# Attention and mixture of experts on one Trainium2 core: how often a place of TensorE's order issues a gather of rows

## The chip, the cores and the metric

One core of a Trainium2 chip runs the whole kernel. The metric is the time of one execution on the device in microseconds. The engines have an instruction stream each and meet through semaphores: TensorE (PE, with its weight loads as PEld), VectorE (DVE), ScalarE (ACT), GpSimd (POOL) and SyncE (SP). GpSimd and SyncE issue the transfers here.

## The reference

Attention over 8 batches of 8 heads of 576 tokens, each with a causal window of 32 (or every fourth of 128), then a mixture of 8 experts in which a token either takes its own best expert or that of the token before it:

```python
attn = softmax(mask(q @ k.T / 8)) @ v                     # B, H, S, D = 8, 8, 576, 64
x = attn.transpose(0, 2, 1, 3).reshape(B, S, 512)
logits = x @ w_gate                                       # 8 experts
local_gate = sigmoid(x @ w_local)
for b in range(B):
    prev_e = -1
    for s in range(S):
        fresh_e = argmax(logits[b, s])
        e = fresh_e if s == 0 or local_gate[b, s] < 0.5 else (prev_e if prev_e >= 0 else fresh_e)
        prev_e = e
        p = softmax(logits[b, s])
        out[b, s] = p[e] * (relu(x[b, s] @ w1[e]) @ w2[e])    # 512 -> 1024 -> 512
```

## The kernel before

Attention comes first and writes the tokens' rows x to device memory, in the tensor xd. The routing then sorts the tokens by expert into tables. The rest of the kernel works through a fixed list of 19 **units**, each a group of tokens of one expert, whose size is the unit's kind: pair (2 x 128 tokens), quad (4 x 128 = 512), full (128), half (64) and quart (32). Units 0 to 3 are pairs; from unit 4 on the list is full, half, **quad (6)**, quart (7), **quad (8)**, full (9), **quad (10)**, half, quart, **quad (13)**, full, **quad (15)**, quart, **quad (17)**, quart.

A unit passes through these steps:

- `weights(u, second)`: SyncE loads the expert's w1 or w2 (2 MB, tile raw, L916) into the slot u % 2, once the unit that held the slot has been through that product. If the expert is the one already held there, the load is skipped.
- `gather(u)` puts the unit's gathers in the list `fetches`; a quad has 16 of them, 4 for each of its 4 tiles xg of 128 tokens. `fetch` issues one: a memset of a single element on VectorE, which claims the tile (L999), then an indirect transfer of 128 rows of 128 values, issued by GpSimd (L1000). There are 9 tiles xg, and `gather_more` puts a unit in the list only when its tiles are free.
- `features(u)`: all gathers of the unit that are still in the list are issued (`fetch_all`); then VectorE transposes each xg into a tile xe (L1037) and forms four sums of those for a quad (tile xcq, L964 to L967).
- `hidden(u)`: the first product. A pair and a quad do it in seven half-size products rather than eight (Strassen's scheme in Winograd's form), for which VectorE forms sums of the weights (tile sum) and afterwards adds parts of the results (L1195 for a quad).
- `output(u)`: the second product (L1293), in the same seven products, once for each half of a quad, with sums of h in the tile hc (L958 to L961). VectorE and ScalarE scale the results by the gate into the tiles y (L1309, L1302, L1306), and GpSimd scatters them to the output (`send`, L1222; L1243 for a half, L1261 for a quart).

The order on TensorE and VectorE is the program's own; no scheduler moves anything there. The main loop runs, for u from 2 on, `hidden(u)`, then `features(u + 1)`, then `output(u - 1)`. `hidden` and `output` are generators that yield at **places** between TensorE's products; a quad's hidden part has 14 places and its output 14. At each place `work_gap` issues up to two pending VectorE operations from the list `soon`, and then `gap(time)` calls `fetch_some(time)`, the credit that sets how often a gather is issued:

```python
def fetch_some(time):
    since[0] = min(since[0] + time, 5)
    cost = 2 if fetches and FIRST <= fetches[0][0] <= TURNED else 3
    if fetches and since[0] >= cost:
        since[0] -= cost
        fetches.pop(0)[1]()
```

For units behind unit 4 a gather costs 3. A place of a pair or a quad gives 2, a place of a smaller unit 1.

Of the kernel before, what the change touches and what calls it, by code (L numbers as in the profile page):

```python
# [218 lines left out]
def whole(ctx, tc, exact, bad, qk, v, wgl, w1, w2, con, msk, qmk, out, cst, wg, ones):  # L219
# [664 lines left out]
    units = [dict(kind="pair", col=2 * i, late=False) for i in range(FIRST)]  # L884
# [15 lines left out]
    def weights(u, second):  # L900

        i = units[u]["slot"]
        loads.add((u, second))
        if not second:
            units[u]["held"] = holds.get(i)
            holds[i] = nc.values_load(of_unit(u, "experts", rows=1), engines=[ET.SP], min_val=0, max_val=E - 1,
                                      skip_runtime_bounds_check_because="clamped to the experts")
            units[u]["expert"] = holds[i]
        e, held = units[u]["expert"], units[u]["held"]
        w, s, pattern = (w2, raw2, "p m f -> p (m f)") if second else (w1[u >= TURNED], raw1, "p m k f -> p (m k f)")  # L910
        if not second and u >= TURNED and units[u]["before"] < TURNED:
            held = None
        if second and not units[u]["late"] and isinstance(held, int):
            held = None
        more = {} if held is None else dict(cond=e != held, cond_hint=False)
        nc.sync.dma_start(out=s[i].rearrange(pattern), in_=w[bass.ds(e, 1)].rearrange("o p x -> (o p) x"), **more)  # L916
# [6 lines left out]
    def next_weights(*did):  # L923

        ready.update(did)
        if "late" in ready:
            for w in [w for w in follow if w in ready]:
                follow.remove(w)
                weights(after[w[0]], w[1])

    def gap(time=3):
        fetch_some(time)
        for steps in waiting, behind:
            if steps:
                f = steps.pop(0)
                if f:
                    f()

    def work_gap(sums=True, time=2):
        for _ in range(len(soon) > 4 and 2 or len(soon) > 0 if sums else 0):  # L940
            soon.pop(0)()
        gap(time)
# [5 lines left out]
    def flush():  # L948
        while soon:
            soon.pop(0)()  # L950
# [18 lines left out]
    def sums_of_weights(u, second):  # L969

        i = units[u]["slot"]
        assert (u, second) in loads
        if second:
            return sums_right(sums[1], *(quarter(raw2[i], k, j, True) for k in range(2) for j in range(2)))
        return sums_left(sums[0], *(quarter(raw1[i], f, k, False) for f in range(2) for k in range(2)))
# [50 lines left out]
    def turn_rows(u):  # L1026
        kind = units[u]["kind"]
        rows = {"half": ROW, "quart": SQ}.get(kind, P)
        assert u >= TURNED or kind == "pair"
        fetch_all(u)  # L1030
        xe[u] = [mw.tile([P, DK, 2 * P], F32, name="xe") for _ in range(2 if kind == "quad" else 1)]
        for j in range({"quad": 4, "pair": 2}.get(kind, 1)):
            x = xg.pop((u, j))
            to = xe[u][j // 2][:, :, j % 2 * P:j % 2 * P + rows]
            if u >= TURNED:
                x = x.rearrange("p g (q f) -> p (g q) f", f=P)
                nc.vector.transpose(to.rearrange("p k (q t) -> p k q t", t=SQ),  # L1037
                                    x[:, :rows // SQ].rearrange("p q (k d) -> p k q d", k=DK))
                continue
            x = x.rearrange("p g f -> p (g f)")  # L1040
            tp = bank([P, DK, P], "tp")
            for kk in range(DK):
                nc.tensor.transpose(tp[:, kk], x[:, kk * P:(kk + 1) * P], ident)
            nc.scalar.copy(to, tp)
# [159 lines left out]
    def turned(u):  # L1204

        h = ht[u]
        n = 2 if units[u]["kind"] == "half" else 1
        ts = h[:, 0:n].rearrange("p m t -> p (m t)")
        tp = bank([P, 2 * n, P], "ht")
        for c in range(2 * n):  # L1210
            nc.tensor.transpose(tp[:, c], ts[:, c * P:(c + 1) * P], ident)
        nc.scalar.copy(h[:, 2:2 + n].rearrange("p m (c t) -> p (m c) t", t=P), tp)
# [244 lines left out]
    def run_hidden(u, push):  # L1457
        soon.extend(push)
        for k, fits in enumerate(hidden(u)):
            work_gap(fits, 2 if is_large(u) else 1)  # L1460
            if u == FIRST and k == 1:
                early_sums[u] = sums_of_weights(u, True)
                soon.extend(early_sums[u][:2])
            if u == FIRST and k == 4:
                turn_rows(u + 1)
        flush()
        if u < FIRST:
            next_weights((u, False))
        elif after[u] is not None:
            weights(after[u], False)  # L1470

    def run_output(u, push):
        soon.extend(push)
        for k, fits in enumerate(output(u)):
            work_gap(fits, 2 if is_large(u) else 1)
            if u == NU - 2 and k == 4:
                turned(u + 1)
        if u == NU - 2 and k < 4:
            turned(u + 1)
        flush()  # L1480
        if u < FIRST:
            next_weights((u, True))
        elif after[u] is not None:
            weights(after[u], True)

    def is_large(u):
        return FIRST <= u < NU and units[u]["kind"] in ("pair", "quad") or 0 <= u < FIRST
# [20 lines left out]

    early_sums[0] = sums_of_weights(0, True)
    run_hidden(0, early_sums[0][:2])  # L1510
    features(1)
    now(both(0))
    run_output(0, [])
    run_hidden(1, sums_of_weights(1, True))
    now(units[1]["sums"])
    fed = False
# [19 lines left out]
    for u in range(FIRST, NU):  # L1536
        own = is_large(u) and u >= TURNED and before_it(u) < u - 1
        run_hidden(u, (both(u - 1) if u > FIRST else []) + (wait(5) + sums_of_weights(u, True) if own else []))
        if u > FIRST and u + 1 < NU:
            features(u + 1)  # L1540
        gather_more(min(u + 1, NU - 1) if u > FIRST else FIRST)
        push = [f for t in when.get(u, []) for f in
                wait((7 if units[u - 1]["kind"] == "quad" else 5) if is_large(u - 1) else 0) + sums_of_weights(t, False)]
        if u > FIRST:
            run_output(u - 1, push)
        else:
            now([f for two_ in zip(sums_of_rows(u + 1), sums_of_weights(u + 1, False)) for f in two_])
        if units[u]["kind"] in ("half", "quart") and u < NU - 1:
            turned(u)
        if u in (FIRST + 3, FIRST + 4) and not exact:  # L1550
            next(checks)
        if u == FIRST + 6 and not exact:
            again = register(bad[0:1, 0:1], 1, "a comparison's result")
    now(both(NU - 1))
    run_output(NU - 1, [])
    return again

# [58 lines left out]
```

## Time and profile before

| | |
|---|---|
| median of 3 runs | 641.37 us (640.75 to 643.07) |
| profiled execution, its own time | 645.84 us |
| span of the profiled execution | 643.9 us |
| PE busy | 604.5 us, 94% of the span |
| PEld busy | 511.2 us, 79% |
| DVE busy | 360.5 us, 56% |
| POOL busy | 226.0 us, 35% |
| ACT busy | 176.2 us, 27% |
| mean granted clock of TensorE | 0.983 of full |
| moved by DMA | 121.18 MB, mean 188 GB/s |

Busy shares are means over stages that are limited by different things. In a row of a timeline stand the start, the duration, the engine, the line and operation, what is written and read, the count of instructions merged in the row, and in square brackets the engine's idle time ahead of it with what ended it. In a row of a stretch of time (A:B) stand its length, then busy time with the count for PE, PEld, DVE, ACT and POOL, then the granted clock, the mean share of the 16 DMA engines, and GB/s; a row for one tile alone leaves out an engine that has nothing to do with it.

### The profile page before, as it was taken

The page shows a single profiled execution, that of the slowest core. Times are in us where ns is not written, and L with a number is a line of the kernel's source. Part 1 is how long each engine was busy: PE and PEld are TensorE (multiplying, and loading weights), DVE is VectorE, ACT ScalarE, POOL GpSimd, SP SyncE. Part 2 cuts the span into 40 slices and gives each one's busy share as a digit, 9 for nine tenths or more (in the row PEclk, how much of TensorE's full clock was granted, in tenths as well). Part 3 has the DMA queues.
Part 4 walks back from the last instruction along what each step waited for, and adds up shares of the span by engine and source line. Part 5 has one row for each costly group of instructions (what it writes and reads, how often), then busy time and mean ns, then how long its engine had stood idle before and what let it go on. Part 6 is the DMA issues. An engine that isn't in the chain of part 4 may idle for free.

```text
span 643.9 us, 13952 instructions
## 1 busy us (share of the span) xinstructions
PE 604.5 (94%) x5678; PEld 511.2 (79%) x5678; DVE 360.5 (56%) x902; ACT 176.2 (27%) x320; POOL 226.0 (35%) x219
## 2 busy tenths in 40 slices
PE   6879988879999998999979999999999999999995
PEld 6767777668888998868768898868789888688884
DVE  3757889989697384374344464434445535443521
ACT  2555544342211331113112311221132113112310
POOL 3232142223014644463256335444543451011011
PEclk8989989999999999999979999999999999999998
DMA  9989988398001247251835192454554650734131
GB/s 348 406 319 294 346 278 299 122 344 342 15 34 35 82 161 262 84 202 26 351 122 188 49 387 76 174 175 164 167 206 160 285 188 31 274 159 163 43 127 42
DMA packets 28442, 121.18 MB, mean 188 GB/s; under 512 B 4748, under 2 KB 15116, under 8 KB 22992
## 3 DMA queue, kind: packets, MB, share of 16 engines
q1 hardware_dynamic: 20800, 101.04, 42.9%
q0 software_dynamic: 7568, 19.15, 8.8%
q8 instruction: 47, 0.77, 0.5%
q14 instruction: 27, 0.22, 0.1%
HBM read 120.17 MB, written 19.14 MB: 216 GB/s over the span
## 4 chain that ended last, share of the span: by engine, by line
PE 79%; DVE 10%; issue 4%; DMA 3%; ACT 1%; POOL 1%; SPq 1%; another core or an unknown queue 0%; DVEq 0%; POOLq 0%
PE yp L1293 29%; PE hp L1179 23%; PE hp L1121 3%; PE pv L410 3%; PE yp L1269 3%; PE hp L1147 3%; PE sc L348 3%; PE hp L1136 2%; PE tp L429 2%; DVE pr L354 2%; DVE x L415 1%; PE yp L1253 1%; PE yp L1234 1%; PE hp L1098 1%; DMA vt<-in_v_dram 1%
## 5 line engine op out<-in xcount | busy, mean ns | idle before, releaser
L1000 POOL DMA_INDIRECT xg<-xd,at x116 | 117.8, 1015 | 144.4 <-DVE xg L999 115.8
L1293 PE MATMUL yp<-sum,hc 128*128 128x256 f32 x384 | 88.7, 380 | 1.6 <-ACT y L1302 1.6
L1293 PEld LDWEIGHTS yp<-sum,hc 128*128 128x128 f32 x384 | 72.7, 190 | 11.8 <-ACT y L1302 2.0
L1222 POOL DMA_INDIRECT out_dram<-y,tok x35 | 43.5, 1242 | 97.3 <-DVE y L1309 43.3
L1309 DVE SCALAR_TENSOR_TENSOR y<-yp,gate,y 128x256 f32<-128x256 f32 x48 | 23.1, 484 | 89.9 <-PE yp L1293 62.1
L1179 PE MATMUL hp<-xcq,sum 128*128 128x256 f32 x288 | 64.1, 379 | 0.0
L1293 PE MATMUL yp<-raw,h 128*128 128x256 f32 x256 | 62.0, 386 | 0.0
L1179 PEld LDWEIGHTS hp<-xcq,sum 128*128 128x128 f32 x288 | 54.7, 190 | 7.4
L357 ACT ACTIVATE pr<-pr 128x512 f32<-128x512 f32 x64 | 43.8, 684 | 60.0 <-DVE pr L354 56.9
L1293 PEld LDWEIGHTS yp<-raw,h 128*128 128x128 f32 x256 | 48.7, 193 | 8.6 <-issue 2.0
L354 DVE SCALAR_TENSOR_TENSOR pr<-sc,mk 128x512 f32<-128x512 f32 x64 | 45.4, 748 | 16.9 <-PE sc L348 15.4
L410 PE MATMUL pv<-vt,pr 128*64 128x65 f32 x1152 | 44.9, 231 | 9.8 <-issue 5.8
L410 PEld LDWEIGHTS pv<-vt,pr 128*64 128x64 f32 x1152 | 39.3, 143 | 13.2 <-issue 7.7
L1195 DVE TENSOR_TENSOR h<-hp,h 128x512 f32<-128x512 f32 x36 | 24.3, 689 | 41.8 <-PE hp L1179 41.8
L1179 PE MATMUL hp<-xe,raw 128*128 128x256 f32 x192 | 43.4, 379 | 0.0
L1179 PEld LDWEIGHTS hp<-xe,raw 128*128 128x128 f32 x192 | 36.2, 190 | 4.8
L1302 ACT ACTIVATE y<-yp,gate 128x256 f32<-128x256 f32 x48 | 22.7, 474 | 61.7 <-PE yp L1293 54.4
L348 PE MATMUL sc<-kq 64*64 64x96 f32 (+3 forms) x1280 | 34.3, 246 | 5.2 <-DVE pr L354 2.8
L289 POOL COPY vt<-vt 64x1040 f32<-64x1040 f32 x16 | 17.3, 1080 | 57.6 <-DMA vt<-in_v_dram 38.8
L348 PEld LDWEIGHTS sc<-kq 64*64 64x64 f32 x1280 | 28.8, 136 | 10.7 <-DVE pr L354 4.0
L1000 POOL DMA_INDIRECT xg<-xd,row x16 | 18.2, 1140 | 52.9 <-DVE xg L999 20.6
L1306 ACT ACTIVATE y<-yp,gate 128x256 f32<-128x256 f32 x16 | 7.6, 475 | 105.7 <-PE yp L1293 105.7
(261 smaller groups left out, 976.6 us busy)
## 6 DMA issues: line engine op xcount, KB each, us to landing
raw<-in_w_dram SPq DMA_DIRECT2D x38, 2048.0 KB
kq<-in_qk_dram SPq DMA_DIRECT2D x13, 1184.0 KB
vt<-in_v_dram SPq DMA_DIRECT2D x15, 650.0 KB
xd<-x SPq DMA_DIRECT2D x16, 512.0 KB
kq<-in_qk_dram SPq DMA_DIRECT2D x6, 592.0 KB
xg<-xd,at POOLq DMA_INDIRECT x116
xd<-x SPq DMA_DIRECT2D x32, 32.0 KB
vt<-in_v_dram SPq DMA_DIRECT2D x2, 325.0 KB
```

The costliest lines, as they stand in the source:

```text
L348: nc.tensor.matmul(sc[c:c + QB, u, lo - a * QB:hi - a * QB], lhsT=kt[h, WIN + j * QB:WIN + (j + 1) * QB], rhs=qt[h, lo:hi], start=True, st ...
L354: nc.vector.scalar_tensor_tensor(to, sc[:, :, :w], -CEIL, mk[:, at:at + w].unsqueeze(1).to_broadcast([P, 2, w]), Alu.max, Alu.min)
L357: nc.scalar.activation(to, to, Act.Exp, scale=SCALE)
L410: nc.tensor.matmul(pv[half * QB:(half + 1) * QB, k - a], lhsT=pr[:, u, (i - a) * QB:(i - a + 1) * QB], rhs=vt[:, slot(i), u], start=True, ...
L1000: nc.gpsimd.indirect_dma_start(out=to, out_offset=None, in_=of, in_offset=bass.IndirectOffsetOnAxis(ap=place, axis=0))
L1121: nc.tensor.matmul(to, lhsT=w[:, m, kk], rhs=x[:, kk, :P], start=(kk == 0), stop=(kk == DK - 1))
L1179: nc.tensor.matmul(to[v][:, m], lhsT=a[:, 2 * v + m, kk], rhs=b[:, kk], start=first and m == 0 and kk == 0, stop=(kk == DK // 2 - 1), skip ...
L1195: nc.vector.tensor_tensor(to, of[v], to, op=Alu.add)
L1222: nc.gpsimd.indirect_dma_start(out=rows_of_out(), out_offset=bass.IndirectOffsetOnAxis(ap=of_unit(u, "tok", j), axis=0), in_=y, in_offset= ...
L1293: nc.tensor.matmul(to, lhsT=a[:, m], rhs=b[:, m], start=first and m == 0, stop=(m == FK // 2 - 1), skip_group_check=True)
L1302: nc.scalar.activation(at(k), of, Act.Copy, scale=of_unit(u, "gate", 2 * s + k // 2))
L1309: nc.vector.scalar_tensor_tensor(at(k), of, of_unit(u, "gate", 2 * s + k // 2), at(k), Alu.mult, Alu.add)
```

## The change

A place of a quad now gives a credit of 3 instead of 2, so that at each of a quad's places one gather is issued while there are any in the list. Places of other kinds are as before.

```diff
     def run_hidden(u, push):
         soon.extend(push)
         for k, fits in enumerate(hidden(u)):
-            work_gap(fits, 2 if is_large(u) else 1)
+            work_gap(fits, 3 if units[u]["kind"] == "quad" else 2 if is_large(u) else 1)
...
     def run_output(u, push):
         soon.extend(push)
         for k, fits in enumerate(output(u)):
-            work_gap(fits, 2 if is_large(u) else 1)
+            work_gap(fits, 3 if units[u]["kind"] == "quad" else 2 if is_large(u) else 1)
```

The order of TensorE, ScalarE and SyncE is the same in both kernels. On VectorE the memsets of L999 move, on GpSimd the gathers of L1000 among the sends. In the rows below a number behind a tile's name tells its buffers apart; they count differently in the two kernels.

VectorE in the second half of unit 6's hidden part (the first quad), before. The tiles xg_3516, xg_3557 and xg_3604 are unit 8's second, third and fourth; xe_3619 is unit 7's.

```order
L999 MEMSET xg_3557 1x1
L967 TENSOR_TENSOR sum_1_2490<-raw2_0_78,sum_1_2490 128x1024
L1195 TENSOR_TENSOR h_3505<-hp_3506,h_3505 128x2x256
L1195 TENSOR_TENSOR h_3505<-hp_3507,h_3505 128x2x256
L999 MEMSET xg_3557 1x1 x2
L1195 TENSOR_TENSOR h_3505<-hp_3508,h_3505 128x2x256
L1195 TENSOR_TENSOR h_3505<-hp_3509,h_3505 128x2x256
L999 MEMSET xg_3604 1x1 x2
L1037 STREAM_TRANSPOSE xe_3619<-xg_3428 128x4x32
L999 MEMSET xg_3604 1x1
```

The same place now; here xg_3545 and xg_3580 are unit 8's third and fourth tiles, and xg_3613 is unit 9's.

```order
L999 MEMSET xg_3545 1x1
L967 TENSOR_TENSOR sum_1_2490<-raw2_0_78,sum_1_2490 128x1024
L999 MEMSET xg_3580 1x1
L1195 TENSOR_TENSOR h_3505<-hp_3506,h_3505 128x2x256
L1195 TENSOR_TENSOR h_3505<-hp_3507,h_3505 128x2x256
L999 MEMSET xg_3580 1x1 x2
L1195 TENSOR_TENSOR h_3505<-hp_3508,h_3505 128x2x256
L1195 TENSOR_TENSOR h_3505<-hp_3509,h_3505 128x2x256
L999 MEMSET xg_3580 1x1
L999 MEMSET xg_3613 1x1 x2
L1037 STREAM_TRANSPOSE xe_3628<-xg_3428 128x4x32
L999 MEMSET xg_3613 1x1 x2
```

Unit 8's last memset now stands right behind unit 6's last L1195, and four of unit 9's follow it. Before, unit 8's fourth tile had three of its four here.

VectorE a little later, at unit 8's `features`, before (xe_3682 and xe_3683 are unit 8's):

```order
L958 TENSOR_TENSOR hc_2492<-h_3505 128x512
L959 TENSOR_TENSOR hc_2492<-hc_2492,h_3505 128x512
L999 MEMSET xg_3604 1x1
L960 TENSOR_TENSOR hc_2492<-h_3505 128x512
L961 TENSOR_TENSOR hc_2492<-h_3505,hc_2492 128x512
L1037 STREAM_TRANSPOSE xe_3682<-xg_3448 128x4x128
L1037 STREAM_TRANSPOSE xe_3682<-xg_3516 128x4x128
L1037 STREAM_TRANSPOSE xe_3683<-xg_3557 128x4x128
L1037 STREAM_TRANSPOSE xe_3683<-xg_3604 128x4x128
```

The same place now:

```order
L958 TENSOR_TENSOR hc_2492<-h_3505 128x512
L959 TENSOR_TENSOR hc_2492<-hc_2492,h_3505 128x512
L960 TENSOR_TENSOR hc_2492<-h_3505 128x512
L961 TENSOR_TENSOR hc_2492<-h_3505,hc_2492 128x512
L1037 STREAM_TRANSPOSE xe_3691<-xg_3448 128x4x128
L1037 STREAM_TRANSPOSE xe_3691<-xg_3516 128x4x128
L1037 STREAM_TRANSPOSE xe_3692<-xg_3545 128x4x128
L1037 STREAM_TRANSPOSE xe_3692<-xg_3580 128x4x128
```

No memset stands between hc's sums any more.

GpSimd over the same stretch, from the end of unit 4's output to unit 6's output, before:

```order
L1000 DMA xg<-xd,at 128x128 x4
L1222 DMA out_dram<-y,tok_2889 4608x512
L1000 DMA xg<-xd,at 128x128 x11
L1243 DMA out_dram<-y,side 9216x256
L1000 DMA xg<-xd,at 128x128 x4
L1222 DMA out_dram<-y,tok_2889 4608x512
```

And now:

```order
L1000 DMA xg<-xd,at 128x128 x4
L1222 DMA out_dram<-y,tok_2889 4608x512
L1000 DMA xg<-xd,at 128x128 x16
L1243 DMA out_dram<-y,side 9216x256
L1000 DMA xg<-xd,at 128x128 x5
L1222 DMA out_dram<-y,tok_2889 4608x512
```

Sixteen gathers are issued ahead of the half unit's scatter (L1243, unit 5) where eleven were; unit 8's last was the first behind that scatter, and is now the twelfth of the sixteen.

VectorE from the weights' sums in unit 6's output to those at the start of unit 8's hidden part, before (the end of that stretch):

```order
L959 TENSOR_TENSOR sum_0_79<-sum_0_79,raw1_0_77 128x1024
L999 MEMSET xg_3762 1x1
L1309 SCALAR_TENSOR_TENSOR y_3756<-yp_3752,gate1_2899,y_3756 128x256
L999 MEMSET xg_3762 1x1
L1309 SCALAR_TENSOR_TENSOR y_3755<-yp_3753,gate1_2899,y_3755 128x256
L960 TENSOR_TENSOR sum_0_79<-raw1_0_77 128x1024
L999 MEMSET xg_3810 1x1
L961 TENSOR_TENSOR sum_0_79<-raw1_0_77,sum_0_79 128x1024
L999 MEMSET xg_3810 1x1 x3
L964 TENSOR_TENSOR sum_1_2490<-raw2_0_78 128x1024
```

And now:

```order
L959 TENSOR_TENSOR sum_0_79<-sum_0_79,raw1_0_77 128x1024
L999 MEMSET xg_3785 1x1
L1309 SCALAR_TENSOR_TENSOR y_3772<-yp_3768,gate1_2899,y_3772 128x256
L999 MEMSET xg_3785 1x1
L1309 SCALAR_TENSOR_TENSOR y_3771<-yp_3769,gate1_2899,y_3771 128x256
L999 MEMSET xg_3819 1x1
L960 TENSOR_TENSOR sum_0_79<-raw1_0_77 128x1024
L999 MEMSET xg_3819 1x1
L961 TENSOR_TENSOR sum_0_79<-raw1_0_77,sum_0_79 128x1024
L999 MEMSET xg_3819 1x1 x2
L999 MEMSET xg_3864 1x1 x2
L999 MEMSET xg_3879 1x1
```

Behind the last row there the sums of L964 follow at once. Nine memsets stand in this stretch where six stood.

## The prediction

> **What bounds the kernel now.** I read the page's first two parts, then the waits of TensorE alone, then the timeline of the one place they name.
>
> ```profile
> span 643.9 us, 13952 instructions
> PE 604.5 (94%) x5678; PEld 511.2 (79%) x5678; DVE 360.5 (56%) x902; ACT 176.2 (27%) x320; POOL 226.0 (35%) x219
> L1000 POOL DMA_INDIRECT xg<-xd,at x116 | 117.8, 1015 | 144.4 <-DVE xg L999 115.8
> ```
>
> TensorE (PE) is busy for 94% of the span. GpSimd (POOL), which issues the gathers (L1000), is busy for 35% and mostly idle ahead of a gather because the mark on VectorE (DVE) ahead of it, the memset of L999, has not yet run. An earlier gather is therefore worth something only where TensorE waits for it. The change acts on units of kind quad, all in the last stage, so I asked what TensorE waited for from 236 us to the end (total us, times, longest), and looked up in the chain of waits where the second of the three stands:
>
> ```profile
> PE yp L1293 <- DVE xg L999: 3.3, 1, 3.3
> PE yp L1293 <- ACT y L1302: 1.6, 1, 1.6
> PE yp L1253 <- issue: 0.3, 1, 0.3
> ```
>
> ```profile
> 243.26 0.48 ACT y L1302
> ```
>
> Three waits in 408 us. The second ends behind this ScalarE copy at 243.7 us, ahead of every quad. The first is the only one of any size behind it, and it is in the output of unit 6, the first quad. TensorE's timeline there, and from the chain of waits the same 112 matmuls of the next quad's output (start, us, what):
>
> ```profile
> 312.59 1.99 PE L1293 MATMUL yp<-raw,h 128*128 128x256 f32 x8
> ...
> 319.60 1.89 PE L1293 MATMUL yp<-sum,hc 128*128 128x256 f32 x8
> 321.33 1.89 PE L1293 MATMUL yp<-raw,hc 128*128 128x256 f32 x8
> 326.50 3.78 PE L1293 MATMUL yp<-sum,h 128*128 128x256 f32 x8 [3.28 <-DVE xg L999]
> 330.08 2.93 PE L1293 MATMUL yp<-raw,h 128*128 128x256 f32 x8
> 332.84 3.62 PE L1293 MATMUL yp<-sum,hc 128*128 128x256 f32 x16
> ...
> 343.20 0.38 PE L1211 MATMUL ht<-cst,h 128*128 128x128 f32 x2
> ```
>
> ```profile
> 377.76 24.18 PE yp L1293 x112
> ```
>
> Unit 6's output takes 343.20 - 312.59 = 30.61 us where the next quad's takes 24.18: 6.43 us are lost at one place. They have two parts. A group of 8 matmuls takes 319.60 to 321.33 = 1.73 us. The idle part is (326.50 - 321.33) - 1.73 = 3.44 us. The next 16 matmuls take 332.84 - 326.50 = 6.34 us instead of 3.46, which is 2.88 us more. The granted clock (the number ahead of the DMA share) says why:
>
> ```profile
> 325.00:326.00 1.00, 0.00 (x0) 0.00 (x0) 1.00 (x4) 0.00 (x0) 0.69 (x2) 0.67 0.04 16
> 331.00:332.00 1.00, 1.00 (x4) 0.81 (x3) 0.00 (x0) 0.00 (x0) 0.70 (x2) 0.50 0.39 148
> 332.00:333.00 1.00, 1.00 (x5) 0.85 (x5) 0.00 (x0) 0.00 (x0) 0.78 (x1) 0.91 0.22 66
> ```
>
> A mean of 0.67 is full clock for a third of that microsecond and half clock behind it, so the clock fell at about 325.3 us, 2.1 us after TensorE stopped (326.50 - 3.28 = 323.2), and came back at about 332.2.
>
> What held TensorE stands on VectorE, which works strictly in its order:
>
> ```profile
> 304.40 0.30 DVE L999 MEMSET xg<- 1x1 f32 x3
> ...
> 312.89 0.06 DVE L999 MEMSET xg<- 1x1 f32 x1
> ...
> 314.08 1.89 DVE L1037 STREAM_TRANSPOSE xe<-xg 128x512 f32<-128x512 f32 x3
> 320.87 0.71 DVE L1037 STREAM_TRANSPOSE xe<-xg 128x512 f32<-128x512 f32 x1 [4.90 <-issue]
> 321.62 0.69 DVE L964 TENSOR_TENSOR xcq<-xe 128x512 f32<-128x512 f32 x1
> ...
> 325.57 0.48 DVE L1309 SCALAR_TENSOR_TENSOR y<-yp,gate,y 128x256 f32<-128x256 f32 x1
> 325.97 0.88 DVE L1309 SCALAR_TENSOR_TENSOR y<-yp,gate,y 128x256 f32<-128x256 f32 x2
> ```
>
> Three of unit 8's four transposes run at once; the fourth stands 4.90 us. Behind it are the sums of unit 8's rows (xcq), two of hc, and the three L1309 that empty unit 6's PSUM. The second L1309 (325.97, done about 326.45) frees the bank into which TensorE's next product goes, at 326.50. The page names no releaser of the 4.90 us ("issue"), so I looked at GpSimd and at the packets of its queue (q0: packets, MB, share), first from 306 to 307, then from 319 to 320 and from 320 to 321 us:
>
> ```profile
> 306.00 0.95 POOL L1000 DMA_INDIRECT xg<-xd,at  x1 [0.30 <-issue]
> 311.60 1.52 POOL L1243 DMA_INDIRECT out_dram<-y,side  x1 [3.40 <-DVE over_any L1449]
> 313.43 0.99 POOL L1000 DMA_INDIRECT xg<-xd,at  x1 [0.30 <-issue]
> 324.52 1.16 POOL L1000 DMA_INDIRECT xg<-xd,at  x1 [10.10 <-DVE xg L999]
> ```
>
> ```profile
> q0 software_dynamic: 32, 0.07, 25.1%
> ...
> q0 software_dynamic: 26, 0.04, 10.9%
> q0 software_dynamic: 1, 0.00, 0.1%
> ```
>
> At 306 us a whole gather (0.07 MB) moves within a microsecond of its issue. The gather issued at 313.43 still has packets between 319 and 320 us, and one behind 320: 7.4 us from issue to the transpose at 320.87. It is unit 8's last, and it runs beside weight loads that fill the DMA engines:
>
> ```profile
> 308.00:316.00 8.00, 0.00 (x0) 0.00 (x0) 1.95 (x4) 1.19 (x2) 1.00 0.99 376
> 316.00:321.00 5.00, 0.00 (x0) 0.00 (x0) 0.13 (x1) 0.00 (x0) 1.00 1.00 419
> ```
>
> (share 0.99 and 1.00, at 376 and 419 GB/s).
>
> **The change part by part.** Nothing is added or removed: TensorE, ScalarE (ACT) and SyncE (SP) keep their order. Each memset with its gather moves up; at a place of a quad one is now due every time instead of two times in three.
>
> *Unit 8's gathers.* By the orders, the last mark of unit 8 moves from behind L959 (312.9 us) to behind unit 6's last L1195, where the memsets of 304.4 us stand. GpSimd has room for it. Seven marks now stand where five stood ahead of the idle 7.33 us, and seven gathers from 285.36 are issued by 297 us even at 1.33 us each with the 0.3 us between two of them, ahead of 299.03:
>
> ```profile
> 285.36 1.33 POOL L1000 DMA_INDIRECT xg<-xd,at  x1 [0.70 <-issue]
> ...
> 299.03 1.69 POOL L1000 DMA_INDIRECT xg<-xd,at  x1 [7.33 <-DVE xg L999]
> ```
>
> So unit 8's last gather goes out at 305 to 306 us, in the place of one of those that GpSimd issued there before, ahead of the burst at 308, and lands by about 307. Even at the crowded 7.4 us it lands at 312.4. The transpose wants it at 315.97 (314.08 + 1.89). The wait goes, by at least 3.5 us of margin.
>
> *What is late next.* With the 4.90 us gone, the second L1309 would start at 325.97 - 4.90 = 321.07; one more memset (0.06 us, by its neighbours' starts 0.1) stands ahead of it, and its product ends only at 321.49 (319.60 + 1.89), so it is done near 322.0. TensorE wants the bank at 323.06 (321.33 + 1.73): 1.1 us to spare, so the idle 3.44 us goes whole. TensorE then has no pause long enough for a lower clock, and the 2.88 us go too. With 0.11 us of rounding: 6.43 us.
>
> The Trainium skill ("TensorE: Matmul & The Clock Gate", Part 1) says that the clock falls to half after at least one idle window of some 3.4 us, and that the window runs freely, so that the place of the fall varies from run to run. Here it fell after 2.1 us, less than the page's figure, and half clock held for 6.9 us, two such windows. By the page an execution may pay the idle alone; that is the first rival.
>
> *Later quads.* Their gathers move up as well. TensorE has no wait on them (the list above), so I cost this at nothing; the cover is the transposes' slack. At the next quad two of them run late too, yet L1309 is there in time, waiting 0.17 us for TensorE:
>
> ```profile
> 379.83 0.71 DVE L1037 STREAM_TRANSPOSE xe<-xg 128x512 f32<-128x512 f32 x1 [1.32 <-DMA xg<-xd,at]
> 384.78 0.48 DVE L1309 SCALAR_TENSOR_TENSOR y<-yp,gate,y 128x256 f32<-128x256 f32 x1 [0.17 <-PE yp L1293]
> ```
>
> *More gathers ahead of sends on GpSimd.* A send (L1222) now stands behind up to two more gathers, 2 x 1.25 = 2.5 us; between nothing and that. The rows of y that it frees are wanted by the next unit, over 10 us on. I take nothing.
>
> *Sum.* The profiled execution took 645.84 us with its span of 643.9; without 6.43 its span is 637.5. It is 4.5 us above the median of the runs shown, so I subtract from the median: 641.37 - 6.43 = 634.9, rounded to 635.0.
>
> **The rivals.** *The idle goes, but the plain runs never paid for the clock.* For it: the profiled execution is 4.5 us slower than the median, and the fall of the clock hangs on where a pause lies. Against: the gather's delay comes from three loads that every run has, and the wait exceeds the 2.1 us by over one. Gain 3.44: 637.9.
>
> *The stall stays, or was the profiled execution's own.* For it: "issue" names no releaser, and 1.1 us is a thin margin for L1309. Against: the packets between 316 and 320 us, and the three transposes ahead, which wrote both xe buffers without waiting. Time 641.4, no change.
>
> *Slower: gathers crowd a quad's second weight load.* At the start of a quad's hidden part VectorE stands for that load:
>
> ```profile
> 351.22 1.23 DVE L964 TENSOR_TENSOR sum<-raw 128x1024 f32<-128x1024 f32 x1 [6.70 <-issue]
> ...
> 355.78 0.69 DVE L1195 TENSOR_TENSOR h<-hp,h 128x512 f32<-128x512 f32 x1 [2.07 <-PE hp L1179]
> ```
>
> Nine gathers now stand between L959 and that L964 where six stood. Three more of 0.07 MB are 0.2 MB, 0.5 us at 419 GB/s. The load may be 2.07 us later before L1195 is late at all, so this decides only if a gather costs more than four times its bytes. If it did at two of the quads, each losing what unit 6 loses now, the time were 641.37 - 6.43 + 2 x 6.43 = 647.8.
>
> **How the numbers follow.** The forecast, 635.0, has 0.58; idle alone, 637.9, 0.20; no change, 641.4, 0.14; slower, 647.8, 0.08. A measurement of this kernel tells about 0.5%, 3.2 us, from no change, so faster is below 638.2: the forecast and 0.14 of the second case, 0.72. Same is 0.14 and the remaining 0.06, 0.20. Slower 0.08. The range: downward 6.43 and the 0.3 us of L1253, less 0.6 for the runs' own spread (641.37 to 640.75): 634.0, set to 633.8. Upward it takes in 637.9 with the runs' spread of 1.7 (643.07 - 641.37), 639.6, and a stall that is only shortened by a little: 640.3. Left out is most of no change and of slower, under 2 in 10.
>
> **What would show it.** In the changed kernel unit 6's output takes about 24.2 us for its 112 matmuls, TensorE's waits behind 240 us hold no L1293 of 3.3, the granted clock is 1.00 from 312 to 344 us, all four transposes of unit 8 run in one row, and q0's packets for them end ahead of the loads near 308. The idle row there with another releaser, or a pause of similar length at a later quad, would prove me wrong; so would an L1195 that waits for VectorE rather than TensorE behind a weight load.

## The result and the profile after

Over seven runs each, the changed kernel takes 634.54 us in the median (632.73 to 637.53) and the kernel before 641.8 (640.72 to 644.71): a ratio of 0.9875 with a 95% interval of 0.985 to 0.990; the two medians alone are 7.3 us apart. Four executions of the runs below, one of them of the kernel before at 1563.12 us, fell in a slower state of the chip, and medians and ratios leave them out. On the 641.37 us of the prediction that is 641.37 x 0.9875 = 633.4, a gain of 8.0 us (6.4 to 9.6), where 6.4 and 635.0 had been forecast. The direction, the place and the mechanism hold; the size lies 0.4 us below the range's low end of 633.8, though the interval, 631.7 to 635.0, takes that end in.

From the page of the changed kernel, the same three rows as before:

```profile
span 630.9 us, 13952 instructions
PE 599.0 (95%) x5678; PEld 508.6 (81%) x5678; DVE 361.3 (57%) x902; ACT 176.3 (28%) x320; POOL 230.0 (36%) x219
L1000 POOL DMA_INDIRECT xg<-xd,at x116 | 124.6, 1074 | 105.7 <-DVE xg L999 78.2
```

TensorE's waits from 236 us to the end had three rows. The same view of the changed kernel has its heading and nothing under it:

```profile
core 0 of [0], span 630.9 us
engine line waited for: us in total, times, longest us
```

TensorE's timeline at unit 6's output (start, us, what) now runs through, group by group at 1.73 us:

```profile
306.44 1.99 PE L1293 MATMUL yp<-raw,h 128*128 128x256 f32 x8
...
315.18 1.89 PE L1293 MATMUL yp<-raw,hc 128*128 128x256 f32 x8
316.91 1.89 PE L1293 MATMUL yp<-sum,h 128*128 128x256 f32 x8
318.63 1.89 PE L1293 MATMUL yp<-raw,h 128*128 128x256 f32 x8
...
330.72 0.38 PE L1211 MATMUL ht<-cst,h 128*128 128x128 f32 x2
```

That is 330.72 - 306.44 = 24.28 us where 30.61 stood. In the stretch from 312 to 344 us the granted clock, behind the five engines, is 1.00:

```profile
312.00:344.00 32.00, 32.00 (x151) 28.15 (x150) 14.25 (x38) 6.55 (x13) 23.64 (x23) 1.00 0.59 221
```

VectorE's timeline holds all four transposes of unit 8 in one row, and the second L1309 now waits for TensorE rather than the reverse:

```profile
307.92 2.48 DVE L1037 STREAM_TRANSPOSE xe<-xg 128x512 f32<-128x512 f32 x4
310.44 0.69 DVE L964 TENSOR_TENSOR xcq<-xe 128x512 f32<-128x512 f32 x1
...
315.45 0.48 DVE L1309 SCALAR_TENSOR_TENSOR y<-yp,gate,y 128x256 f32<-128x256 f32 x1 [0.57 <-PE yp L1293]
```

GpSimd's timeline, with the load of the DMA engines behind it (stretches of three microseconds; share and GB/s stand last):

```profile
298.62 0.94 POOL L1000 DMA_INDIRECT xg<-xd,at  x1 [0.30 <-DVE xg L999]
...
303.61 0.94 POOL L1000 DMA_INDIRECT xg<-xd,at  x1 [0.30 <-issue]
305.45 1.52 POOL L1243 DMA_INDIRECT out_dram<-y,side  x1 [0.90 <-DVE over_any L1449]
```

```profile
300.00:303.00 3.00, 3.00 (x25) 1.96 (x25) 0.00 (x0) 0.60 (x1) 2.39 (x3) 1.00 0.66 131
303.00:306.00 3.00, 3.00 (x46) 1.72 (x46) 1.28 (x5) 0.00 (x0) 1.79 (x3) 1.00 0.83 345
```

The row of 303.61 is the sixteenth gather ahead of the half unit's scatter (L1243), and unit 8's last, the twelfth, is the row of 298.62, ahead of the loads, with which the share is 0.83 between 303 and 306 us.

The two profiled spans differ by 13.0 us, twice what the change did. Up to unit 6's hidden part the two programs are the same, yet it starts 6.15 us apart, as the chain of waits shows, first before, then after:

```profile
283.01 24.18 PE hp L1179 x112
```

```profile
276.86 24.18 PE hp L1179 x112
```

Of the 13.0 us, 6.15 are this difference of the stage ahead, 6.33 are unit 6's output, and 0.5 are all the rest. In the next four profiles on that view, two of them of these two kernels again and all with the same code up to there, the start lies at 276.74 to 280.09 us, so the 6.15 us are not counted as the change's.

### The profile page after: what moved, and what is told of

It is laid out like the page before. It is cut to its first block, busy times and chain, and to the rows that moved or that the text cites. A ratio compares the mean times of both kernels' runs of the same rounds, so it can differ in the third digit from the quotient of the medians.

```text
span 630.9 us, 13952 instructions
## 1 busy us (share of the span) xinstructions
PE 599.0 (95%) x5678; PEld 508.6 (81%) x5678; DVE 361.3 (57%) x902; ACT 176.3 (28%) x320; POOL 230.0 (36%) x219
## 4 chain that ended last, share of the span: by engine, by line
PE 83%; DVE 10%; issue 3%; DMA 2%; POOL 0%; ACT 0%; SPq 0%; DVEq 0%; POOLq 0%
PE yp L1293 31%; PE hp L1179 23%; PE hp L1147 4%; PE pv L410 4%; PE hp L1121 3%; PE yp L1269 3%; PE sc L348 3%; DVE pr L354 2%; PE hp L1136 2%; PE tp L429 2%; DVE x L415 2%; PE yp L1253 1%; PE hp L1108 1%; PE yp L1234 1%; PE hp L1098 1%
## 5 line engine op out<-in xcount | busy, mean ns | idle before, releaser
L1000 POOL DMA_INDIRECT xg<-xd,at x116 | 124.6, 1074 | 105.7 <-DVE xg L999 78.2
L1222 POOL DMA_INDIRECT out_dram<-y,tok x35 | 40.6, 1159 | 113.6 <-DVE y L1272 44.9
L1309 DVE SCALAR_TENSOR_TENSOR y<-yp,gate,y 128x256 f32<-128x256 f32 x48 | 23.2, 484 | 87.4 <-PE yp L1293 50.4
L1195 DVE TENSOR_TENSOR h<-hp,h 128x512 f32<-128x512 f32 x36 | 24.3, 688 | 42.8 <-PE hp L1179 42.8
L1302 ACT ACTIVATE y<-yp,gate 128x256 f32<-128x256 f32 x48 | 22.8, 474 | 61.4 <-PE yp L1293 58.9
L1000 POOL DMA_INDIRECT xg<-xd,row x16 | 18.2, 1138 | 50.0 <-DVE xg L999 20.6
```

What stands on the lines that cost most here:

```text
L1000: nc.gpsimd.indirect_dma_start(out=to, out_offset=None, in_=of, in_offset=bass.IndirectOffsetOnAxis(ap=place, axis=0))
L1195: nc.vector.tensor_tensor(to, of[v], to, op=Alu.add)
L1222: nc.gpsimd.indirect_dma_start(out=rows_of_out(), out_offset=bass.IndirectOffsetOnAxis(ap=of_unit(u, "tok", j), axis=0), in_=y, in_offset= ...
L1302: nc.scalar.activation(at(k), of, Act.Copy, scale=of_unit(u, "gate", 2 * s + k // 2))
L1309: nc.vector.scalar_tensor_tensor(at(k), of, of_unit(u, "gate", 2 * s + k // 2), at(k), Alu.mult, Alu.add)
```

## The experiments

Theory one is the prediction's: the whole gain is unit 8's last gather, which was issued into the burst of weight loads. The rivals were that other quads' gathers gain too, that the stall had another cause, and that more or fewer gathers would have done better. Each ratio is to the kernel before, run on the same chip in the same batch.

**The two kernels once more.**

> The changed kernel as it is. Theory one (the whole gain is the stall at unit 6's output): 6.4 us less than before, ratio 0.990, and from unit 6's first product to the end a span shorter by 6.3 to 6.8 us; what was measured beyond that comes from the stage ahead of unit 6, where the two programs are the same. Rival (the later quads' earlier gathers add to it): ratio 0.9875 again, 8 us, and a gain behind unit 8's start in the trace.

> The kernel before against itself. All theories: ratio 1.000 within 0.3%. Theory one: its profile shows unit 6's output at 30 to 31 us for the 112 matmuls again, with a pause of about 3.3 us and half clock behind it. Rival (the stall was that execution's own): 24.2 us there and no pause. The start of unit 6's hidden part will tell how much the stage ahead differs between executions of one program; it was 282.85 us in the first profile.

Measured: the changed kernel 635.24 us, ratio 0.9884 (0.9856 to 0.9912). The kernel before against itself 0.9983 (0.9958 to 1.0009), so 0.2% are within what identical code shows. The second profile of before has the stall again, with another size:

```profile
PE yp L1293 <- DVE xg L999: 3.9, 1, 3.9
```

```profile
318.41 1.89 PE L1293 MATMUL yp<-raw,hc 128*128 128x256 f32 x8
324.19 3.78 PE L1293 MATMUL yp<-sum,h 128*128 128x256 f32 x8 [3.89 <-DVE xg L999]
...
330.63 3.62 PE L1293 MATMUL yp<-sum,hc 128*128 128x256 f32 x16
```

By the prediction's working the idle part is (324.19 - 318.41) - 1.73 = 4.05 us and the half clock costs (330.63 - 324.19) - 3.46 = 2.98. The stall stands in both profiled executions of before, so it was not the first one's own; its 6.43 us were one draw.

**The change at unit 6 alone, and everywhere but there.** First the kernel before with the new credit in unit 6's hidden part only:

```diff
-            work_gap(fits, 2 if is_large(u) else 1)
+            work_gap(fits, 3 if u == 6 else 2 if is_large(u) else 1)
```

> The credit of 3 in unit 6's hidden part alone, 2 at all other places of large units. Theory one: the same time as the changed kernel within 0.2%, 6.4 us below before (ratio 0.990). Rival (the later quads add to it): 1 to 2 us slower than the changed kernel.

Measured: 635.05 us, ratio 0.9879 (0.9852 to 0.9906), the same as the whole change. Its VectorE:

```profile
310.70 2.48 DVE L1037 STREAM_TRANSPOSE xe<-xg 128x512 f32<-128x512 f32 x4
```

Then the changed kernel without unit 6's hidden part:

```diff
-            work_gap(fits, 3 if units[u]["kind"] == "quad" else 2 if is_large(u) else 1)
+            work_gap(fits, 3 if units[u]["kind"] == "quad" and u != 6 else 2 if is_large(u) else 1)
```

> The credit of 3 at every quad's places except those of unit 6's hidden part. Theory one: the time of before within 0.2% (ratio 1.000), and the pause of 3.3 us at unit 6's output stands. Rival (the later quads add to it): 1 to 2 us faster than before (0.997).

Measured: 641.68 us, ratio 0.9999 (0.9976 to 1.0022), nothing. The stall is whole; on VectorE and on TensorE:

```profile
315.58 0.71 DVE L1037 STREAM_TRANSPOSE xe<-xg 128x512 f32<-128x512 f32 x1 [5.51 <-issue]
```

```profile
315.43 1.89 PE L1293 MATMUL yp<-raw,hc 128*128 128x256 f32 x8
321.23 3.26 PE L1293 MATMUL yp<-sum,h 128*128 128x256 f32 x8 [3.91 <-DVE xg L999]
...
326.47 3.62 PE L1293 MATMUL yp<-sum,hc 128*128 128x256 f32 x16
```

Idle 5.80 - 1.73 = 4.07 us, half clock 5.24 - 3.46 = 1.78 us. So the gain is made in one hidden part of one unit, and the other quads' earlier gathers are worth nothing, as the prediction had it.

**One gather held back.** The changed kernel, with unit 8's last gather alone issued at the start of `features(8)`. All else stays early.

```diff
+                if (u, j, q) == (8, 3, NQS - 1):
+                    held_back.append(one)
...
+        if u == 8:
+            while fetches and fetches[0][0] < 8:
+                fetches.pop(0)[1]()
+            for f in held_back:
+                f()
```

> The changed kernel, but unit 8's sixteenth and last gather alone is held back to the start of unit 8's features, some 1.2 us behind where it stood before the change; the other gathers are early as in the changed kernel. Theory one (that single gather, caught in the burst of weight loads, is the whole stall): the stall is back, the fourth transpose waits 5 to 7 us, unit 6's output takes 30 to 32 us, and the time is that of before or up to 1.5 us above it (ratio 1.000 to 1.003). Rival (it is the number of early gathers that counts, or VectorE's marks among its other work): most of the gain stays, ratio below 0.993.

Measured: 648.4 us, ratio 1.0024 (1.0009 to 1.0039). The whole gain is gone, by one gather of 116. Its GpSimd and VectorE (the added lines shift L1000 to L1004 and L1037 to L1046):

```profile
314.54 0.98 POOL L1004 DMA_INDIRECT xg<-xd,at  x1 [1.64 <-DVE xg L1003]
```

```profile
321.37 0.71 DVE L1046 STREAM_TRANSPOSE xe<-xg 128x512 f32<-128x512 f32 x1 [5.62 <-DMA xg<-xd,at]
```

Here the releaser, which the profile of before only calls "issue", is named: the gather. It takes 6.83 us to its transpose.

**The loads taken away instead.** The kernel before, with its late gather, but without two of the three loads that it met: unit 7's second weights and unit 9's first are not loaded.

```diff
+        if (u, second) in ((7, True), (9, False)):
+            return
```

> The kernel before, but the loads of unit 7's second weights and of unit 9's first weights are left out (those units then multiply with what lies in the slot, so their rows of the output are other ones). Unit 8's last gather is issued as late as before. Theory one (the gather is late because it shares the DMA engines with the loads): with one load of three left the engines are free by about 6 us after the burst's start, the gather lands about 2 to 3 us behind its issue, and the pause shrinks to under 0.5 us or goes: ratio 0.989 to 0.992. Rival (a gather issued there is late by its own latency or by GpSimd): the fourth transpose still waits about 5 us, ratio 1.000.

Measured: 640.65 us, ratio 0.9901 (0.9877 to 0.9926). The gather is issued at the same time as before, and its transpose runs 3.6 us behind it instead of 7.4; in the stretch from 316 to 321 us the DMA engines now stand still where they moved 419 GB/s:

```profile
313.42 0.98 POOL L1002 DMA_INDIRECT xg<-xd,at  x1 [0.30 <-issue]
```

```profile
317.01 0.71 DVE L1039 STREAM_TRANSPOSE xe<-xg 128x512 f32<-128x512 f32 x1 [1.05 <-issue]
```

```profile
316.00:321.00 5.00, 5.00 (x25) 4.41 (x24) 3.91 (x7) 0.95 (x2) 0.34 (x1) 1.00 0.00 0
```

TensorE has no wait there any more. A late gather without two of the three loads costs nothing, and so does an early one with all of them: what cost was the two together.

**The idle and the clock apart.** The kernel before, with matmuls on constants put ahead of the product that waits, in unit 6's first output half; 24 of them, then 12. They hold off no data; they keep TensorE from standing still.

```diff
+        def filler():
+            to = bank([P, P], "warm")
+            for _ in range(24):
+                nc.tensor.matmul(to, lhsT=ones, rhs=ones, start=True, stop=True)
```

> The kernel before, with 24 matmuls of 128 x 128 on the tile of ones put ahead of the product that stands in unit 6's output; their result is not used. They last about 24 x 0.112 = 2.7 us, inside the pause of 3.3 to 3.9 us. Theory one (the clock falls because TensorE pauses there): the wait on VectorE ends where it did, the granted clock stays at 1.00, and 1.8 to 2.9 us are gained: ratio 0.9955 to 0.9972. Rival (the clock falls for another reason): no gain, ratio 1.000, half clock still behind the pause.

Measured: 646.01 us, ratio 0.9982 (0.9963 to 1.0000). The 24 cost twice what had been reckoned, and each stands as two records:

```profile
322.50 5.52 PE L1318 MATMUL warm<-ones 128*128 128x128 f32 x48
327.86 1.89 PE L1295 MATMUL yp<-sum,h 128*128 128x256 f32 x8
```

On VectorE the copies that free the bank (L1309, here L1311; the second of them done about 326.56) are ready before that:

```profile
326.08 0.88 DVE L1311 SCALAR_TENSOR_TENSOR y<-yp,gate,y 128x256 f32<-128x256 f32 x2
```

So the 24 outlast the pause by some 1.3 us, and give back as much of what the full clock saves. Hence the 12:

```diff
-            for _ in range(24):
+            for _ in range(12):
```

> As busy_in_the_pause with 12 matmuls instead of 24: there the 24 took 5.4 us, 0.223 each, and outlasted the pause by 1.3 us. Twelve take 2.7 us. Theory one: TensorE stands for about 0.6 to 1.2 us behind them, the granted clock stays at 1.00, and 1.7 to 2.9 us are gained over before: ratio 0.9955 to 0.9975. Rival (the clock's fall costs nothing of its own): ratio 1.000.

Measured: 643.46 us, ratio 0.9966 (0.9942 to 0.9990). The matmuls are over before the bank comes free, and the clock stays at 1.00 in the microsecond where it had been 0.67:

```profile
322.27 2.84 PE L1318 MATMUL warm<-ones 128*128 128x128 f32 x24
326.43 1.99 PE L1295 MATMUL yp<-sum,h 128*128 128x256 f32 x8 [1.32 <-DVE xg L999]
```

```profile
325.00:326.00 1.00, 0.11 (x2) 0.00 (x0) 1.00 (x4) 0.00 (x0) 0.69 (x2) 1.00 0.00 0
```

So the clock's share is a cost of its own, 0.34% or 2.2 us here (0.6 to 3.7), and it can be had without touching the wait.

**More gathers.** If one gather per place is good, are two better? The changed kernel with a second one at each place of a quad:

```diff
+            if units[u]["kind"] == "quad":
+                fetch_some(3)
```

> The changed kernel with two gathers at each of a quad's places instead of one, as long as any are in the list. Theory one (only unit 8's gathers are on the path): the time of the changed kernel within 0.3%, ratio 0.988 to 0.991. Rival (gathers crowd a quad's second weight load, or hold the sends up on GpSimd): L964 waits longer for its load than 6.8 us, TensorE pauses behind it at one or more quads, and the time is 2 us or more above the changed kernel's.

Measured: 674.56 us, ratio 1.0449 (1.041 to 1.0488), a loss of 29 us against the kernel before. The rival had a loss, but not by this way: VectorE's waits for the second weights of units 8, 10, 15 and 17 (L964) are 6.1, 6.0, 7.5 and 6.9 us, where the changed kernel has 6.8, 6.3, 7.2 and 6.9. TensorE's waits behind 236 us:

```profile
PE yp L1293 <- ACT y L1302: 11.3, 3, 6.8
PE yp L1293 <- issue: 4.9, 2, 2.9
PE hp L1179 <- issue: 4.1, 1, 4.1
PE yp L1293 <- DVE y L1309: 2.1, 2, 1.7
```

The longest of them, on GpSimd, ScalarE, TensorE and VectorE:

```profile
333.55 3.62 PE L1293 MATMUL yp<-sum,hc 128*128 128x256 f32 x16
337.00 1.89 PE L1293 MATMUL yp<-raw,h 128*128 128x256 f32 x8
...
339.43 1.02 POOL L1222 DMA_INDIRECT out_dram<-y,tok  x1 [0.30 <-issue]
...
345.17 0.47 ACT L1302 ACTIVATE y<-yp,gate 128x256 f32<-128x256 f32 x1 [6.59 <-remote]
345.69 3.78 PE L1293 MATMUL yp<-sum,hc 128*128 128x256 f32 x8 [6.80 <-ACT y L1302]
...
351.61 0.48 DVE L1309 SCALAR_TENSOR_TENSOR y<-yp,gate,y 128x256 f32<-128x256 f32 x1 [18.33 <-remote]
```

A send (L1222) stands behind ten gathers. ScalarE's copy into y at 345.17 empties the second of the two products in the row of 333.55, whose records end at 337.17; it starts 8.0 us behind that, where in the changed kernel the same copy starts within 0.1 us. I read this as tiles y that are not free because their sends are late, and gave y six buffers in place of four, at each place where it is made:

```diff
-        ys = [stage.tile([P, D], F32, name="y", bufs=4) for _ in range(2)]
+        ys = [stage.tile([P, D], F32, name="y", bufs=6) for _ in range(2)]
```

> Two gathers at each of a quad's places as in the kernel two_per_place, but six tiles y instead of four. There the sends of a quad's results stood behind up to eleven gathers on GpSimd, and ScalarE and VectorE waited to write y. Theory one (the loss is the wait for a tile y whose send is late): with six tiles most of the loss goes, at least 20 of the 28 us, ratio below 1.015. Rival (the loss comes from somewhere else, as the gathers' transfers themselves or a semaphore shared by gathers and sends): the loss stays, ratio 1.03 to 1.05.

Measured: 675.06 us, ratio 1.045 (1.0405 to 1.0496). Nothing changed; that theory fell.

The events that the traces have of TensorE's semaphore, by which it reports a finished product, say more. Of the changed kernel's 42 L1302 behind 236 us, 38 start some 24 ns behind such an event and the others within 74 ns. In the kernel with two per place, the copy at 345.17 waits for that semaphore alone, and starts 23 ns behind its event of 345.14. So ScalarE waited for no tile y, but for the report of a product. It seems to be the report that was late, not the product: VectorE's L1309 at 351.61 takes the product of 337.00, which ends at 338.89 by its records, and starts 12.7 us later, though TensorE, which goes in its order, has by then been through the next product as well (345.69). In the changed kernel that L1309 starts 0.1 us behind its product. The trace with two per place lacks some of these events (it has 474 where 490 matmuls give one), so this is a reading of the rows that it has.

Next the density: a second gather at every other place, 1.5 per place.

```diff
+            if units[u]["kind"] == "quad" and k % 2:
+                fetch_some(3)
```

> Between the changed kernel and two_per_place: at every second place of a quad two gathers, at the others one. Eight gathers instead of five stand ahead of the first send of unit 6's output. Theory one (a late send costs only once the tiles y run out): below two_per_place by far, between the changed kernel's time and 10 us above it, ratio 0.988 to 1.005. Rival (every further gather ahead of a send costs its own 1.25 us): about half of two_per_place's loss, ratio 1.015 to 1.02.

Measured: 668.6 us, ratio 1.0341 (1.0298 to 1.0384); against the changed kernel four fifths of the loss (0.047 of 0.057) at half of the surplus. Last, a second gather at every fourth place:

```diff
+            if units[u]["kind"] == "quad" and k % 4 == 3:
+                fetch_some(3)
```

> At every fourth place of a quad a second gather is issued, 1.25 per place on the mean, where 1.5 and 2 per place made the kernel 3.4% and 4.5% slower. A gather takes GpSimd 0.95 us and 0.30 us stand between two, so 1.25 gathers take 1.56 us of a place's 1.73: GpSimd keeps up, where 1.5 (1.88 us) and 2 (2.50 us) leave it behind. Theory A, that the loss comes only where GpSimd falls behind and issues without a pause for many microseconds: as the changed kernel, ratio 0.985 to 0.99, no idle time of TensorE ended by ScalarE at L1302 in the quads. Theory B, that any gathers ahead of the changed kernel's take memory or semaphores that others need, whatever GpSimd's pauses: a part of the loss by density, a quarter of that of 2 per place against the changed kernel, (1.045 - 0.988) / 4 = 0.014, so a ratio near 1.00.

Measured: 634.21 us, ratio 0.986 (0.9803 to 0.9916), as the changed kernel. TensorE has no wait behind 236 us:

```profile
core 0 of [0], span 634.5 us
engine line waited for: us in total, times, longest us
```

So the loss sets in between 1.25 and 1.5 gathers per place, and between the two GpSimd's 1.25 us for a gather (0.95 and 0.30 between two) come to exceed a place's 1.73: 1.56 us are asked of it at 1.25 and 1.88 at 1.5. That the one causes the other is not shown. It is not the unbroken row as such. GpSimd's timeline of this kernel has 24 transfers with no longer pause than 0.31 us between two, the first and the last of them being these, and it pays nothing:

```profile
372.63 1.21 POOL L1000 DMA_INDIRECT xg<-xd,at  x1 [9.93 <-DVE xg L999]
...
404.56 0.94 POOL L1000 DMA_INDIRECT xg<-xd,at  x1 [0.30 <-issue]
```

What holds TensorE's reports back at that density is not shown by any of these runs. The loss stays open in its mechanism; only the density at which it sets in is known. None of these kernels beats the changed one by more than the interval.

## Why the prediction was right, and where it was not

- **The wait and its cause: right.** Taking away the gather's lateness (the change, unit 6 alone) or the loads (two left out) removes the stall; putting one gather back restores it.
- **Where the gather goes: right.** Forecast at 305 to 306 us; it is issued at 298.62, which with the 6.15 us of the stage ahead added is 304.8.
- **What is late next: right.** The second L1309 was given 1.1 us to spare; it now waits 0.57 us for TensorE and is done at 315.93, 1.0 us ahead of 316.91, and no wait of TensorE is left.
- **Later quads worth nothing: right.** 0.9999 for the change without unit 6's hidden part.
- **Sends behind gathers cost nothing: right at this density only.** At 1.5 and 2 gathers per place the kernel is 3.4 and 4.5% slower than before. Six tiles y did not help, so it is no wait for a tile whose send is late; the rest is open.
- **The rivals.** Idle alone falls: the changed kernel's clock stays at 1.00, and the clock's share was measured by itself. No change falls. Gathers crowding the second weight load: it did not come. VectorE waits for that load as before, and its next L1195 for TensorE:

```profile
338.93 1.23 DVE L964 TENSOR_TENSOR sum<-raw 128x1024 f32<-128x1024 f32 x1 [6.83 <-DMA raw<-in_w_dram]
...
343.30 0.69 DVE L1195 TENSOR_TENSOR h<-hp,h 128x512 f32<-128x512 f32 x1 [1.88 <-PE hp L1179]
```

- **The step that failed is the range's low end: "downward 6.43 and the 0.3 us of L1253, less 0.6 for the runs' own spread".** It took the stall of one execution as fixed and allowed 0.6 us for the runs, from the three runs at hand; with the 0.3 and the rounding to 633.8 the low end lay 1.1 us below the sum. The mis-sized term is that allowance: the ratio of seven runs against seven is known to 1.6 us each way, and the stall itself is 5.9 to 7.0 us. In the four profiled executions that have it, it is (unit 6's output less 24.28), with what the trace has of the granted clock beside it:

| | idle us | half clock costs us | stall us | clock falls, us behind TensorE's stop | half clock lasts us |
|---|---|---|---|---|---|
| before, of the prediction | 3.44 | 2.88 | 6.33 | 2.1 | 6.83 |
| before, once more | 4.05 | 2.98 | 7.04 | 2.9 | 6.83 |
| all but unit 6 | 4.07 | 1.78 | 5.86 | 4.5 | 3.41 |
| one gather held back | 4.66 | 1.68 | 6.35 | 4.3 | 3.41 |

Half clock lasts 3.41 us or twice that in these four. It begins early or late in the pause, once 0.6 us behind its end, and the longest pause paid least. The mean of the stall is 6.4, and the forecast's centre was sound for profiled executions.

Whether the plain runs gain more than 6.43 us is less sure. The ratios of the whole change and of unit 6 alone, 0.9875, 0.9884 and 0.9879, give 7.4 to 8.0 us, or 633.4 to 633.9, on both sides of the low end; the medians lie 6.8 to 7.3 us apart. So it was partly chance that the time fell outside.

The plain runs also hint at which part of the stall is larger. Each has its span and its mean granted clock; span x (1 - clock) is what the lower clock took, and the rest is everything else. In the batch with both kernels run once more, 22 runs of before have 10.3 us of clock and 629.8 of rest on the mean, and six of the changed kernel 6.2 and 626.8 (each to about 0.5). So 3.0 us are gained in the rest and 4.1 in the clock. Half clock also covers 1.2 us in which TensorE stood idle (325.3 to 326.5 in the prediction's execution), which cost nothing by the clock: 0.6 us belong to the other side. That makes 3.6 us of idle, where 3.44 had been taken, and 3.5 of clock, where 2.88 had: 7.1 us in all, a ratio of 0.989. This points to the half clock, but does not show it. The 3.5 are known to some 0.7 us; the 12 matmuls in the pause gained 2.2 (0.6 to 3.7); half of 6.83 us is 3.4, and no trace has a longer stretch of half clock there; and the mean clock takes in the stage ahead, where the same code had two to four stretches of 3.41 us at half clock in these traces.

The Trainium skill ("TensorE: Matmul & The Clock Gate", Part 1) says that the window runs freely, so that the place of the fall varies from run to run; the four executions agree, with 1.7 to 3.0 us for pauses of 3.4 to 4.7 us, and the longest pause paid least. I had cited that rule for a smaller gain only, as a rival; it speaks for a spread on both sides.

## What to carry to other kernels

Where one wait is all that an almost full engine has, ask what else uses the transfer's path in the microseconds in which it is issued: here 64 KB of rows took 6.8 to 8.1 us from issue to their reader beside three weight loads and 3.6 with two of the three left out, and moving the one issue ahead of the burst gave the whole gain. A pause of TensorE of 3 to 5 us cost more than its length here, and the part that the clock adds differs from run to run, so a gain read from one execution needs that spread on both sides. Try how far issuing ahead may go: a quarter more gathers were free here, half more lost, against the changed kernel, some four times what the change had gained, and why is open.

## What was not expected of the hardware

- A 128 x 128 by 128 matmul on f32 constants stands as two records, and takes (5.52 - 2.84) / 12 = 0.22 us.
- Matmuls over 2.84 us of a pause of some 4 us keep the clock at 1.00; the 1.3 us that stay idle don't lower it.
- Behind a pause of 3.4 to 4.7 us the half clock lasts 3.41 us or twice that, and begins 2.1 to 4.5 us behind TensorE's stop.
- With GpSimd asked for 1.88 us of work or more per 1.73 us, 22 to 29 us are lost against the kernel before, and at 2.50 us per 1.73 the reports of TensorE's products seem to come up to 12.7 us behind the end of their records; with 1.56 us per 1.73 neither shows.
